# Attention mixer with a four-batch feed-forward: sums of weight blocks distributed over four chunks, in pieces of 256 columns, and three of four early weight loads moved behind a branch

## The chip, the cores and the metric

The kernel runs on one core of one Trainium2 chip. The metric is the device time of one execution in microseconds (us). Three runs of the kernel before gave 744.5, 745.9 and 746.22 us; their median, 745.9 us, is the time before.

## The reference, cut to what matters

```
# attention: q, k, v are [4, 8, 768, 64]; a row sees 4 sink columns and the last 128
scores = where(is_sink | in_window, 0.125 * q @ k.T, -1e9)
x = softmax(scores) @ v                      # heads joined: [4, 768, 512]
# token mixing over the sequence, U [768, 32], V [32, 768]
u = x + ((x.transpose(0, 2, 1) @ U) @ V).transpose(0, 2, 1)
# feed-forward, w_ch1 [512, 2048], w_ch2 [2048, 512]
out = u + relu(u @ w_ch1) @ w_ch2            # all in float32
```

U, V and the weights reach the kernel as 64-bit floats and are narrowed to float32 on the chip.

## The kernel before, in words

The batches go through TensorE one after the other. The attention of batch 0 comes first, alone; then the feed-forward of batch b runs while the attention and the token mixing of batch b+1 are fitted in between its matmuls. Each batch has two chunks of 384 rows, and (b, c) below is chunk c of batch b. A chunk has 16 steps, one for each block f of 128 columns of the hidden layer: 12 matmuls of the first layer (L1251 to L1253) and 9 of the second (L1272). Every operand is split into a high and a low part (two narrow floats whose sum is the float32 value), which is why each product is three matmuls. Chunk 0 takes the blocks in the order 15 to 0, chunk 1 in the order 0 to 15.

Weights: in batch 0 each weight piece (128 x 512 of 64-bit floats) is loaded into one of four `big` buffers, narrowed in seven operations on VectorE (DVE), ScalarE (ACT) or GpSimd (POOL) (`narrow_steps`, L107 to L117), split into high and low parts in a weight tile `w`, and written to DRAM (`wd`). Later chunks fetch `w` from `wd` (1 MB each) into four slots used in turn; blocks 0 and 8 stay resident. A slot gets its next block when all readers of the old one are done.

Batch 3 uses a seven-product scheme (as in Strassen's) for the first layer (`ffn_last`, L1139). It needs, for each pair j of blocks (2j, 2j+1), four combinations of the weights. They are made ahead, in `sums` (L1083 to L1102), while batches 1 and 2 run, and kept in DRAM (`sd`). One sum is: two additions of 128 x 512 that put high and low part of a block together again (L1088, recorded under the helper's lines L514 for DVE and L516 for POOL), four additions or subtractions of 128 x 256 (L1095), one rounding copy of 128 x 1024 (L1097, recorded under L507 for ACT and L508 for DVE), one subtraction of 128 x 1024 for the low part (L1098), and two DMAs of 512 KB to `sd`. Its two tiles `a` and `t` are two of the four `big` buffers, which the output tiles of the chunks use too, strictly in turn. The table `SUMS` (L41) says in which chunk a pair is made; it happens at the step where both blocks of the pair have been fetched.

The order of all instructions on all queues is worked out at build time by a planner (`Plan`): a list scheduler that places some thousands of steps by priority with a cost for each, repeats this with priorities from a backward pass, then tries a few random disturbances (one for each entry of `SEEDS`) and keeps the order with the shortest planned span. SyncE (SP) issues the DMAs in that order and waits at each for what it needs.

Before the planned part the kernel issues some loads by hand (L1579 to L1588): the limits, k and q of the first two head pairs of batch 0, and four weight pieces into the four `big` buffers: U, the two halves of V and the first piece of block 0. Then a branch on the limits chooses between the fast and a general version. What stands behind the branch, the loads of k, q and v of the third head pair and all others included, is issued after it. `narrow` (L525) takes an early buffer if there is one, and otherwise issues a load of its own.

Of the kernel before, what the change touches and what calls it, by code (L numbers as in the profile page):

```python
# [15 lines left out]
U16 = mybir.dt.uint16  # L16
AF = mybir.ActivationFunctionType
ALU = mybir.AluOpType
# [8 lines left out]
DM = H * D  # L27
# [11 lines left out]
K2 = DM // 2  # L39
NPF = NF // 2  # L40
SUMS = {(1, 1): (0, 1, 2, 3), (2, 0): (7, 6, 5, 4)}  # L41
NEG = 8.0e9
# [6 lines left out]
TURNS = 4  # L49
SEEDS = (300012, 300023, 300026,)  # L50
SLACK = 0.0344
# [5 lines left out]
NSTREAM = 4  # L57
NBIG = 4
NNR = 6
NHH = 2  # L60
# [23 lines left out]
def f32(ap):  # L84
    return ap.bitcast(F32)
# [163 lines left out]
class Plan:  # L249
# [116 lines left out]
    def forward(self):  # L366
        avail = dict.fromkeys(self.SYNC, 0.0)
        ready = {e: [] for e in avail}
        dma = port = 0.0

# [33 lines left out]
        while done < len(self.steps):  # L404
# [8 lines left out]
            if pick is None:  # L413
                t, e = turn[0]
                pick = min((s for s in ready[e] if at(s, e) <= t + 1e-9), key=lambda s: (s.prio, s.n))
            s = pick
# [6 lines left out]
            if lock:  # L423
                port = t + s.dur
            avail[e] = t + s.dur
            end = t + s.dur + s.lat
            if e == "SP" and s.lat < 0.0:
                end = -s.lat
                dma = max(dma, end - 1.3)
            elif e == "SP":  # L430
                dma = max(dma, t + s.dur + 0.65) + s.lat
                end = dma + 1.3
# [47 lines left out]
class Fast:  # L480
# [44 lines left out]
    def narrow(self, src, n, prio, dst=()):  # L525

        raw, A, S_ = self.raw(), self.nr(), self.nr()
        if len(self.early) > 0:
            self.early.pop(0)
            self.plan.add("SP", 0.0, lambda: None, w=(raw,), lat=-EARLY[NBIG - 1 - len(self.early)], prio=-1e6)  # L530
        else:
            self.put(raw, lambda: (raw().bitcast(U16)[:, 1:4 * n + 1], src), P * n * 8, prio - 8.0)
        x = self.bank() if dst else None
# [3 lines left out]
        for i, ((ways, r, w), c) in enumerate(zip(steps, cost)):  # L537
            r, w = (box[r],) if r else (), box[w]
            if x and i >= 5:
                r, w = r + (w,), x  # L540
# [542 lines left out]
    def sums(self, j, ws, prio):  # L1083

        a, t = self.raw(), self.raw()
# [10 lines left out]
        hi, lo = (lambda x=x: x()[:, :2 * DM].bitcast(F32R) for x in (a, t))  # L1096
        self.copy(2 * DM, hi, ft, r=(t,), w=(a,), prio=prio)  # L1097
        self.tt(2 * DM, lo, ft, lambda: f32(hi()), ALU.subtract, r=(a,), w=(t,), prio=prio)  # L1098
        sd = self.sd[j]
        for i, (x, y) in enumerate(((a, hi), (t, lo))):  # L1100
            self.put(sd, lambda i=i, y=y: (f32(sd()[:, 2 * i:2 * i + 2].rearrange("p a n -> p (a n)")), f32(y())), 1 << 19, prio,
                     r=(x,), part=i)  # L1102
# [460 lines left out]
def sink_attention_mixer(ctx, tc, q, k, v, vs, limits, U, V, w1, w2, out):  # L1563
# [5 lines left out]
    with tc.tile_pool(name="work", bufs=1) as work, tc.tile_pool(name="idle", bufs=1, space=PSUM) as idle, \  # L1569
# [16 lines left out]
        for src, n in ((U, NB * RANK), (V[0], VC), (V[1], VC), (w1[ORDER[0]], DM))[:NBIG]:  # L1586
            early.append(pre.tile([P, RAW], I32, name=f"big{len(early)}"))
            nc.sync.dma_start(early[-1].bitcast(U16)[:, 1:4 * n + 1], src)  # L1588
        tri = sp.tile([P, 2, P], F32, name="tri")
# [69 lines left out]
```

## Time and profile before

| | |
|---|---|
| median of three runs | 745.9 us |
| the profiled execution | 747.41 us |
| its span, from the first to the last instruction | 745.7 us |
| TensorE (PE) busy | 725.6 us, 97% of the span |
| VectorE (DVE) busy | 494.8 us, 66% |
| ScalarE (ACT) busy | 369.6 us, 50% |
| GpSimd (POOL) busy | 219.8 us, 29% |
| moved by DMA | 157.34 MB, 211 GB/s on average |

In the span the attention of batch 0 fills the first 70 us, batch 0's feed-forward lies from 70.5 to 254.0 us, the chunks (1,0), (1,1), (2,0) and (2,1) begin at 253.96, 345.24, 432.41 and 528.53 us, and batch 3 begins at 612.30 us. Times in all views count from the start of the span. A matmul's recorded duration contains its way through the array, so matmuls that follow one another overlap in the records, and an engine that is busy all the time by the records need not run at its full pace.

### The profile page before, as it was taken

The numbers are of one execution on the slowest core, as the hardware profiler recorded it, in microseconds if no ns is written. First come the engines' busy times: TensorE is split into PE (matmuls) and PEld (weight loads), VectorE is DVE, ScalarE is ACT, GpSimd is POOL, SyncE is SP. The second block draws the span as 40 slices with busy tenths as digits, with TensorE's granted clock in tenths as the row PEclk, the third lists the DMA queues.
The fourth block names the chain that finished last, engine by engine and source line by source line (L and its number), as shares of the span: only waits on it lengthen the run. The fifth ranks groups of instructions, "written<-read, shape, count | busy, mean of one in ns | idle before, by whom it ended". The sixth has DMA issues, their size and how long they took to land.

```text
span 745.7 us, 11814 instructions
## 1 busy us (share of the span) xinstructions
PE 725.6 (97%) x4032; PEld 626.5 (84%) x4032; DVE 494.8 (66%) x1209; ACT 369.6 (50%) x1029; POOL 219.8 (29%) x337
## 2 busy tenths in 40 slices
PE   8989999999998999999999999999999999999997
PEld 7757877778787999999879998898998989888895
DVE  6899889897899567677975198975667224122233
ACT  5996475775874455555543165654545113121220
POOL 4751040313731153353811055754422000000000
PEclk9999999999999999999999999999999999999999
DMA  7559667765795378663599448984157734366433
GB/s 240 157 181 337 245 238 243 267 239 220 227 288 231 129 218 288 185 211 95 171 332 321 173 141 244 350 278 124 72 183 254 239 129 156 133 236 262 173 113 118
DMA packets 46373, 157.34 MB, mean 211 GB/s; under 512 B 5728, under 2 KB 12512, under 8 KB 36576
## 3 DMA queue, kind: packets, MB, share of 16 engines
q1 hardware_dynamic: 46016, 156.11, 61.7%
q8 instruction: 34, 0.56, 0.3%
q10 hardware_dynamic: 288, 0.39, 0.2%
q14 instruction: 35, 0.29, 0.1%
HBM read 116.37 MB, written 40.11 MB: 210 GB/s over the span
## 4 chain that ended last, share of the span: by engine, by line
PE 78%; DVE 9%; ACT 6%; DMA 4%; issue 2%; POOL 2%; SPq 0%; ACTq 0%; DVEq 0%; POOLq 0%
PE bank L1272 23%; PE bank L1209 9%; PE bank L1251 8%; PE bank L1139 8%; PE bank L1252 8%; PE bank L1253 7%; PE bank L693 2%; PE bank L840 2%; PE bank L791 2%; PE bank L717 2%; ACT p L749 1%; PE bank L737 1%; DMA qkraw<-in_q_dram 1%; PE bank L738 1%; DMA v_raw<-in_v_dram 1%
## 5 line engine op out<-in xcount | busy, mean ns | idle before, releaser
L1272 PE MATMUL bank<-w,hh 128*128 128x512 f32 x576 | 184.1, 401 | 0.0
L1251 PE MATMUL bank<-ul,w 128*128 128x384 f32 x384 | 134.2, 350 | 0.7 <-ACT w L507 0.5
L1252 PE MATMUL bank<-uh,w 128*128 128x384 f32 x384 | 129.3, 337 | 0.4 <-DVE w L514 0.3
L1253 PE MATMUL bank<-uh,w 128*128 128x384 f32 x384 | 129.2, 336 | 0.0
L1272 PEld LDWEIGHTS bank<-w,hh 128*128 128x128 f32 x576 | 103.6, 188 | 17.0 <-issue 2.4
L1272 PE MATMUL bank<-w,hl 128*128 128x512 f32 x288 | 114.2, 396 | 1.9 <-DVE hl L1262 1.9
L1262 DVE SCALAR_TENSOR_TENSOR hl<-bank,hh 128x384 fp32r<-128x384 f32 x96 | 53.0, 552 | 58.7 <-ACT hh L1259 58.0
L1259 ACT ACTIVATE hh<-bank 128x384 fp32r<-128x384 f32 x90 | 44.1, 490 | 92.7 <-PE bank L1253 92.2
L749 ACT ACTIVATE p<-p,ms 128x132 f32<-128x132 f32 (+1 forms) x144 | 70.0, 487 | 33.6 <-DVE ms L746 33.4
L1251 PEld LDWEIGHTS bank<-ul,w 128*128 128x128 f32 x384 | 72.4, 188 | 9.4 <-issue 3.4
L1252 PEld LDWEIGHTS bank<-uh,w 128*128 128x128 f32 x384 | 72.3, 188 | 5.1 <-DVE w L514 1.4
L1253 PEld LDWEIGHTS bank<-uh,w 128*128 128x128 f32 x384 | 72.2, 188 | 0.0
L1272 PEld LDWEIGHTS bank<-w,hl 128*128 128x128 f32 x288 | 54.1, 188 | 15.5 <-DVE hl L1262 3.1
L746 DVE CUSTOM_DVE_ANT_0 p<-bank,mask 128x132 f32<-128x132 f32 (+1 forms) x144 | 54.1, 400 | 14.6 <-PE bank L738 9.7
L516 POOL TENSOR_TENSOR p<-p 128x256 f32<-128x256 f32 (+1 forms) x26 | 21.0, 806 | 76.3 <-ACT p L749 75.2
L1170 DVE TENSOR_TENSOR qkraw<-bank,p 128x384 f32<-128x384 f32 x12 | 6.7, 557 | 54.9 <-PE bank L1139 54.9
L1209 PE MATMUL bank<-w,ul 128*128 128x512 f32 x144 | 39.7, 394 | 0.0
L516 POOL TENSOR_TENSOR ul<-xT,uh 128x384 fp32r<-128x384 f32 x9 | 9.1, 1026 | 83.2 <-ACT uh L507 51.7
L507 ACT COPY p<-bank 128x384 f32<-128x384 f32 x16 | 7.7, 478 | 52.0 <-PE bank L1139 52.0
L1209 PEld LDWEIGHTS bank<-w,ul 128*128 128x128 f32 x144 | 26.9, 187 | 6.0
L817 POOL TENSOR_SCALAR_AFFINE_SELECT oph<-oph 128x384 fp32r<-128x384 f32 (+1 forms) x48 | 28.0, 583 | 5.9 <-ACT oph L507 3.1
L791 PE MATMUL bank<-ident,p 128*128 128x128 f32 x144 | 25.8, 279 | 3.6 <-ACT p L773 2.7
(261 smaller groups left out, 1570.2 us busy)
## 6 DMA issues: line engine op xcount, KB each, us to landing
w<-wd SPq DMA_DIRECT2D x52, 1024.0 KB, 5.4
big<-in_w_dram SPq DMA_DIRECT2D x32, 512.0 KB, 4.5
wd<-w SPq DMA_DIRECT2D x16, 1024.0 KB, 4.6
big<-xd SPq DMA_DIRECT2D x33, 256.0 KB, 3.2
sd<-big SPq DMA_DIRECT2D x16, 512.0 KB, 7.2
w<-sd SPq DMA_DIRECT2D x8, 1024.0 KB, 5.0
qkraw<-in_k_dram SPq DMA_DIRECT2D x32, 198.0 KB, 5.5
qkraw<-in_q_dram SPq DMA_DIRECT2D x32, 192.0 KB, 4.6
```

Of the source, the lines that this page charges most:

```text
L516: ways["POOL"] = (gps(n), lambda: nc.gpsimd.tensor_tensor(dst(), a(), b(), op), True)
L746: add("DVE", dve(wd), lambda: nc.vector.tensor_tensor_reduce(p()[:, u, NS + lo:], st()[:, :wd], self.mask[:, min(qb, 2), lo:], -0.125, 3.0 ...
L749: add("ACT", act(wd) + 0.22, lambda: nc.scalar.activation(p()[:, u, NS + lo:], p()[:, u, NS + lo:], AF.Exp, bias=sm()[:, j:j + 1], scale=-1.0,
L791: nc.tensor.transpose(tr()[:, u * P:(u + 1) * P], p()[:, u, SW + NS:], self.ident)
L1139: nc.tensor.matmul(out(), stat(p, dd), mv(dd), start=first and dd == 0 and k == 0, stop=dd == 1 and k == 2, skip_group_check=True)
L1209: nc.tensor.matmul(accs[k](), a()[:, sl], w()[:, m, :], start=False, stop=n == NPF - 1 and f == 1 and q == 2)
L1251: nc.tensor.matmul(ph()[:, :CH], wh, ul()[:, d, :], start=d == 0, stop=False)
L1252: nc.tensor.matmul(ph()[:, :CH], wl, uh()[:, d, :], start=False, stop=False)
L1253: nc.tensor.matmul(ph()[:, :CH], wh, uh()[:, d, :], start=False, stop=d == NC - 1)
L1259: self.plan.any({"ACT": (act(CH), lambda: nc.scalar.activation(hh(), ph()[:, :CH], AF.Relu)), "DVE": (dve(CH), lambda: nc.vector.tensor_sc ...
L1262: add("DVE", dve(CH), lambda: nc.vector.scalar_tensor_tensor(hl(), ph()[:, :CH], 0.0, f32(hh()), ALU.max, ALU.subtract), r=(ph, hh), w=(hl ...
L1272: nc.tensor.matmul(acc[k](), a()[:, sl], w()[:, m, :], start=not begin and i == 0 and j == 0, stop=i == n - 1 and j == 2)
```

## The change

`SUMS` is (1,0): pairs 7, 6; (1,1): pairs 2, 3; (2,0): pairs 5, 4; (2,1): pairs 0, 1, where it was four pairs in (1,1) and four in (2,0). The rounding copy and the low-part subtraction of a sum are four pieces of 256 columns each, with dependencies for each piece, where each was one instruction of 1024 columns. Of the four weight pieces ahead of the branch only U is still loaded there; the loads of both halves of V and of the first piece of block 0 are ordinary planned loads behind it. The planner counts the DMA time of the early loads from its start, and it tries two other seeds in place of three.

```diff
-SUMS = {(1, 1): (0, 1, 2, 3), (2, 0): (7, 6, 5, 4)}
+SUMS = {(1, 0): (7, 6), (1, 1): (2, 3), (2, 0): (5, 4), (2, 1): (0, 1)}
...
-SEEDS = (300012, 300023, 300026,)
+SEEDS = (100004, 100009,)
...
+NEARLY = 1
...
     def forward(self):
...
-        dma = port = 0.0
+        port = 0.0
+        dma = max((-s.lat - 1.3 for s in self.steps if s.lat < 0.0), default=0.0)
...
             if e == "SP" and s.lat < 0.0:
                 end = -s.lat
-                dma = max(dma, end - 1.3)
...
     def narrow(self, src, n, prio, dst=()):
...
-        if len(self.early) > 0:
+        if len(self.early) > NBIG - NEARLY:
...
     def sums(self, j, ws, prio):
...
-        self.copy(2 * DM, hi, ft, r=(t,), w=(a,), prio=prio)
-        self.tt(2 * DM, lo, ft, lambda: f32(hi()), ALU.subtract, r=(a,), w=(t,), prio=prio)
+        for i in range(4):
+            h, l, x = (lambda i=i, v=v: v()[:, i * K2:(i + 1) * K2] for v in (hi, lo, ft))
+            self.copy(K2, h, x, r=[(t, i)], w=((a, i // 2),), prio=prio)
+            self.tt(K2, l, x, lambda h=h: f32(h()), ALU.subtract, r=[(a, i // 2)], w=((t, i),), prio=prio)
...
             early.append(pre.tile([P, RAW], I32, name=f"big{len(early)}"))
-            nc.sync.dma_start(early[-1].bitcast(U16)[:, 1:4 * n + 1], src)
+            if len(early) <= NEARLY:
+                nc.sync.dma_start(early[-1].bitcast(U16)[:, 1:4 * n + 1], src)
```

## Rows read from the trace of the kernel before

**Rows 1.** The page's first two parts: busy time of each engine, and the busy share of DVE in 40 equal slices of 18.6 us.

```profile
PE 725.6 (97%) x4032; PEld 626.5 (84%) x4032; DVE 494.8 (66%) x1209; ACT 369.6 (50%) x1029; POOL 219.8 (29%) x337
...
DVE  6899889897899567677975198975667224122233
```

**Rows 2.** The timeline of PE at the first first-layer matmul of the chunks (1,0), (1,1), (2,0), (2,1) and of batch 3: start, duration, engine, line.

```profile
253.96 0.34 PE L1251 MATMUL bank<-ul,w 128*128 128x384 f32 x1
...
345.24 0.34 PE L1251 MATMUL bank<-ul,w 128*128 128x384 f32 x1
...
432.41 0.34 PE L1251 MATMUL bank<-ul,w 128*128 128x384 f32 x1
...
528.53 0.42 PE L1251 MATMUL bank<-ul,w 128*128 128x384 f32 x1
...
612.30 0.51 PE L1139 MATMUL bank<-kh,w 128*128 128x384 f32 x2
```

**Rows 3.** The busy time of each engine in stretches: start:end and length, then PE, PEld, DVE, ACT, POOL busy with the number of instructions, the granted clock, DMA share and GB/s. The stretches are batch 0's feed-forward and the chunks (1,0), (1,1), (2,0), (2,1).

```profile
70.50:254.00 183.50, 179.45 (x985) 145.92 (x985) 157.94 (x375) 113.08 (x290) 51.41 (x71) 1.00 0.70 241
254.00:345.20 91.20, 91.20 (x544) 84.13 (x543) 65.13 (x180) 53.27 (x174) 37.32 (x70) 1.00 0.62 196
345.20:432.40 87.20, 84.88 (x453) 75.34 (x452) 55.77 (x104) 34.28 (x80) 26.61 (x31) 1.00 0.68 231
432.40:528.50 96.10, 93.82 (x543) 83.79 (x542) 77.81 (x195) 57.28 (x181) 52.19 (x75) 1.00 0.70 221
528.50:612.30 83.80, 83.80 (x456) 75.88 (x455) 41.51 (x85) 29.57 (x69) 18.66 (x28) 1.00 0.55 189
```

**Rows 4.** Who PE waited for, in the chunk (1,1) and then in (2,0): total us, times, longest.

```profile
PE bank L953 <- ACT first1q L507: 0.7, 1, 0.7
PE bank L791 <- ACT p L773: 0.5, 1, 0.5
PE bank L976 <- ACT big L507: 0.5, 1, 0.5
PE bank L936 <- DVE xT L939: 0.4, 1, 0.4
...
PE bank L840 <- POOL oph L817: 1.2, 2, 1.0
PE bank L791 <- ACT p L773: 1.1, 2, 0.9
```

**Rows 5.** The same view as in rows 3 for parts of these chunks: the two parts of (1,1), the two parts of (2,0), and the first part of (2,1).

```profile
345.20:382.00 36.80, 34.69 (x203) 30.21 (x201) 33.19 (x65) 20.16 (x53) 21.31 (x26) 1.00 0.65 210
382.00:432.40 50.40, 50.19 (x252) 45.12 (x251) 22.58 (x40) 14.12 (x28) 5.30 (x5) 1.00 0.71 247
432.40:480.00 47.60, 46.49 (x269) 40.86 (x268) 44.57 (x111) 30.70 (x97) 28.43 (x39) 1.00 0.80 261
480.00:528.50 48.50, 47.33 (x276) 42.94 (x275) 33.23 (x84) 26.57 (x85) 23.76 (x37) 1.00 0.59 181
528.50:580.00 51.50, 51.50 (x295) 47.02 (x294) 35.66 (x75) 25.63 (x61) 16.99 (x27) 1.00 0.55 190
```

**Rows 6.** Groups of instructions by line, engine and shape: count, busy us in total, mean ns of one, idle time before them. The first two are instructions of the sums over the whole span; the next two are two more of the sums, in (1,1) alone; the last is ACT's copy of 384 columns, from 345.2 to 528.5 us.

```profile
L514 DVE TENSOR_TENSOR big<-big,big 128x1024 fp32r<-128x1024 f32 x6 | 7.8, 1292 | 0.2 <-ACT big L507 0.2
...
L507 ACT CAST big<-big 128x1024 fp32r<-128x1024 f32 x6 | 6.3, 1048 | 8.6 <-DVE big L514 5.5 <-POOL opl L814 2.5 <-POOL big L516 0.5
...
L514 DVE TENSOR_TENSOR big<-big,big 128x256 f32<-128x256 f32 x6 | 2.5, 418 | 0.1
L516 POOL TENSOR_TENSOR big<-big,big 128x1024 fp32r<-128x1024 f32 x1 | 2.4, 2402 | 0.0
...
L507 ACT CAST oph<-bank 128x384 fp32r<-128x384 f32 x16 | 7.6, 475 | 3.2 <-PE bank L791 3.1
```

**Rows 7.** DMA issues in (1,0) and then in (2,0): destination and source, count, KB each, median us from issue to landing.

```profile
w<-wd SPq DMA_DIRECT2D x10, 1024.0 KB, 5.2
...
w<-wd SPq DMA_DIRECT2D x10, 1024.0 KB, 7.9
sd<-big SPq DMA_DIRECT2D x8, 512.0 KB, 6.9
```

**Rows 8.** The timeline of SP's DMA issues at the start: start, us until the last of the row was issued, queue, line, destination and source.

```profile
2.67 0.91 SPq L1588 DMA_DIRECT2D big<-in_V_dram  x2
4.18 0.33 SPq L1588 DMA_DIRECT2D big<-in_w_dram  x1
6.34 0.33 SPq L522 DMA_DIRECT2D kh<-in_k_dram  x1
6.73 0.43 SPq L522 DMA_DIRECT2D qs<-in_q_dram  x1
```

**Rows 9.** DMA issues of the first 12 us and then of 13 to 29 us, as in rows 7.

```profile
big<-in_V_dram SPq DMA_DIRECT2D x2, 384.0 KB, 5.5
big<-in_w_dram SPq DMA_DIRECT2D x1, 512.0 KB, 6.0
...
qs<-in_q_dram SPq DMA_DIRECT2D x2, 192.0 KB, 4.7
...
qs<-in_q_dram SPq DMA_DIRECT2D x4, 192.0 KB, 2.9
```

**Rows 10.** The timelines of PE, DVE and ACT where the third head pair of batch 0 begins; in brackets the idle time before and what ended it.

```profile
11.42 2.54 PE L693 MATMUL bank<-kh,qs 64*128 64x132 f32 x12 [1.93 <-ACT p L749]
...
12.20 0.29 DVE L746 CUSTOM_DVE_ANT_0 p<-bank,mask 128x132 f32<-128x132 f32 x1 [1.81 <-PE bank L693]
...
12.65 1.00 ACT L773 ACTIVATE qkraw<-qkraw,r 128x132 f32<-128x132 f32 x3 [1.35 <-DVE r L760]
```

**Rows 11.** The same view as in rows 3 for two stretches of batch 0's attention.

```profile
10.00:15.00 5.00, 3.58 (x17) 2.87 (x18) 3.00 (x20) 3.28 (x14) 2.15 (x5) 0.66 0.87 283
20.00:40.00 20.00, 20.00 (x164) 15.10 (x159) 17.93 (x70) 19.43 (x71) 13.82 (x26) 1.00 0.48 150
```

**Rows 12.** The timeline of DVE at the first reads of the two halves of V and of the first piece of block 0.

```profile
25.62 0.35 DVE L108 TENSOR_SCALAR nr<-big 128x384 uint16<-128x384 uint16 x1
...
37.08 0.35 DVE L108 TENSOR_SCALAR nr<-big 128x384 uint16<-128x384 uint16 x1
...
44.41 0.42 DVE L108 TENSOR_SCALAR nr<-big 128x512 uint16<-128x512 uint16 x1
```

## The prediction

> **What bounds the kernel now.** The page comes first: PE is busy in 97% of the span, and the slices in which DVE is at 8 or 9 tenths lie in the first third, around 350 to 370 us and around 440 to 480 us [rows 1]. So PE sets the time, and a change to DVE, ACT, POOL or DMA work is worth only what it takes from PE's waits. Busy time does not show all of these, because records of matmuls overlap. The better measure here is how long equal PE work takes. The chunks (1,0) and (2,0) do the same work, 544 and 543 matmuls, and last 91.2 and 96.1 us; (1,1) and (2,1) do 453 and 456 and last 87.2 and 83.8 us [rows 2, 3]. The two longer ones are those that hold four sums each. The difference, 4.9 + 3.4 = 8.3 us, is my price of the eight sums as they are placed now, about 1.04 us each. The list of waits agrees in place: PE idles 2.1 us in (1,1) and 2.3 us in (2,0) behind ACT, DVE and POOL work, and in the two chunks without sums it is busy throughout [rows 3, 4]. The rest of the 8.3 us is pace lost under overlapping records. Within (1,1) the loss is all in the first 36.8 us, where the attention and mixing of batch 2 end and DVE is busy 33.2 us; after that DVE is busy 22.6 of 50.4 us [rows 5]. In (2,0) DVE is busy 44.6 of the first 47.6 us [rows 5]. The DMA queue is slower there too: a weight fetch lands 7.9 us after its issue, against 5.2 us in (1,0) [rows 7].
>
> The second limit is the start. Until 70.5 us PE waits on a chain of DVE and ACT work. In it the third head pair begins at 11.42 us after PE idled 1.93 us, DVE 1.81 us, and ACT 1.35 us soon after [rows 10]. The view names ACT as the releaser, but this matmul reads only k and q and needs a PSUM bank that DVE frees. The q load, issued at 6.73 us [rows 8] with 4.7 us to landing [rows 9], lands at 11.4 us, which is when PE starts. So this is a wait for a DMA.
>
> **Part 1, the early loads.** V's two halves (2 x 384 KB) and the first piece of block 0 (512 KB) leave the queue ahead of that k and q. They are issued at 2.67 to 4.5 us [rows 8] and land 5.5 and 6.0 us later, the last about 10.2 us [rows 9]. Loads of the same q size take 2.9 us when less stands ahead [rows 9], so q would land at 6.73 + 2.9 = 9.6 us, 1.8 us earlier. DVE was free at 12.20 - 1.81 = 10.39 us and ACT at 12.65 - 1.35 = 11.30 us [rows 10], so DVE can gain up to 1.81 and ACT 1.35 us. From 20 to 40 us ACT is the fuller of the two, busy 19.43 of 20 us [rows 11], so I take ACT's 1.35 us as what reaches the end of the stage; bounds 0 (the rest of the chain waits for something else) and 1.8 us. PE's granted clock is 0.66 from 10 to 15 us [rows 11], that is partly at the lower of its two levels, after this idle time; less idle time may spare this too, which I don't count. Behind 70.5 us DVE is busy 157.9 of 183.5 us and PE 179.5 [rows 3], so the shift passes through to PE's work.
>
> The three loads are now planned, so SP issues three more DMAs behind the branch, 0.43 us each by its q issue [rows 8]. They can stand behind the k, q and v of the third and fourth pair, and whoever is queued behind them on SP gets its load up to 1.3 us later. Their readers come at 25.6, 37.1 and 44.4 us [rows 12], and even with 6.0 us to landing an issue by 19 us is in time for the first. So I cost them at nothing, under the cover of the attention work up to 25 us; without this cover each us of lateness would be one of DVE's chain. The Trainium skill's page "DMA: Bandwidth & Descriptors", section "Rules for kernel authors", says the opposite of this part: issue a DMA early and wait on it late, so that its fixed cost overlaps. By it the part gains nothing, which is rival D below. The rows speak against it, because these transfers have 15 us or more to spare while a load that is needed at once stands behind them.
>
> **Part 2, where the sums lie.** The work of a sum does not change, its place does. (1,1) keeps the pairs 2 and 3, whose blocks come at its steps 4 to 7. With 87.2 / 16 = 5.45 us a step the first of these pairs is complete at about 345.2 + 5 x 5.45 = 372 us, so most of the work falls into the part where DVE is busy under half of the time [rows 5]: I take 0.5 us for both, against 3.4 now. (2,1) gets two at its start; DVE is busy 35.7 of its first 51.5 us [rows 5], so there is room, but batch 3's mixing lies there: 0.8 us. (1,0) and (2,0) hold two each, at DVE loads between 65.1 in 91.2 us (cost nothing) and 77.8 in 96.1 us (cost 4.9) [rows 3]. If the cost grew in proportion, two sums would cost 2.45 us; if with the square, 1.2. I take 1.85 each, in the middle. New price 0.5 + 0.8 + 1.85 + 1.85 = 5.0 us, gain 8.3 - 5.0 = 3.3 us; bounds 0 (the price stays 1.04 us a sum wherever it lies) and 8.3 us. The change also makes the output tiles of (1,0) and (2,1) wait, on SP, for `big` buffers that sums hold until their DMAs have landed (6.9 us each [rows 7]). These tiles are needed at the chunk's end, some 50 us after the sums, so the feed-forward covers that and I cost it at nothing.
>
> **Part 3, the pieces.** Each sum has three more copies and three more subtractions, 24 of each in all. A 256-column operation takes 418 ns on DVE, so four take 1.67 us against 1.29 us for the one of 1024 columns: +0.38 us [rows 6]. For the copy no 256-column row exists; on ACT it lies between a quarter of 1.05 us and the 0.475 us of 384 columns [rows 6], so four cost between nothing and 0.85 us more; I take 0.35. Eight sums make 8 x 0.73 = 5.8 us of engine time. The sums of (2,0) are 12.7 us of DVE, 4.0 of ACT and 14.9 of POOL, by the differences to (1,0), and cost PE 4.9 us: 0.155 us for one us of engine time [rows 3]. That makes 0.9 us. On the other side a piece frees the engine sooner: now a subtraction of 2.40 us stands on POOL as one block [rows 6], in front of the masks that PE waits for. I take +0.4 us, bounds -0.5 and +0.9. What hides the rest is the feed-forward's matmuls.
>
> The Trainium skill's page "VectorE: DVE Perf Modes", section on the TRN2 errata, speaks against this part: SBUF-source operations pay a fixed cost per instruction, so tile at 512 elements or more. The trace agrees in the price of one (4 x 418 against 1292 ns); if DVE were the bound, this alone would be 8 x 0.38 = 3.0 us, and the sum below would end at 744.2.
>
> **Part 4, the planner.** Other seeds and start values give another order everywhere. No row prices it; it can move small waits either way, and I widen the range by 1.5 us on both sides and add nothing to the sum.
>
> **Sum.** -1.35 - 3.3 + 0.4 = -4.25 us. The profiled execution took 747.41 us with a span of 745.7, so the same execution would come to 743.2. The median of the three runs, 745.9 us, lies 1.5 below it; against the median the forecast is 741.6 us.
>
> **The rivals.** (A) The price of the sums nearly vanishes, because it was only crowding: then -1.8 - 6.9 + 0.2 (the gain of part 2 at 1.4 us left), about 737.5 us. For it: the waits sit in the crowded stretches alone. Against: (1,0) and (2,0) stay fuller than (1,0) is today. (B) The load moves and its price with it: the waits of (2,0) reappear in (1,0), the pieces cost their 0.9 us, and only the start gains: 745.9 - 1.35 + 0.9 = 745.5 us. For it: DVE, ACT and POOL do more work than before. Against: the DVE load of (1,0) would stay below today's of (2,0). (C) Slower: in (1,0) the slots of the blocks 15 to 12 come free only when the additions of the pairs 7 and 6 have read them, and these now queue behind the end of batch 0's narrowing and batch 2's attention. A step is 91.2 / 16 = 5.7 us, the fifth block is needed at about 254 + 4 x 5.7 = 277 us, and its fetch takes 5.2 us or, at today's load of (2,0), 7.9 [rows 3, 7]. From an addition later than 269 us on, each us is one of PE. Four additions that are 2 us late each cost 8 us, against the gain of the start and half of that of part 2: 745.9 + 8 - 1.35 - 1.65 + 0.4 = 751.3 us. Against: in (2,0) the same pairs have the same slots today, and no wait on `w` is in its list [rows 4]. (D) The start gains nothing, because the three loads, once planned, stand in the way of other loads of the attention or reach their readers late: 745.9 - 3.3 + 0.4 = 743.0 us. For it: the DMA share from 10 to 15 us is 0.87 already [rows 11]. Against: from 20 to 40 us it is 0.48, and the readers come late [rows 11, 12].
>
> **How the numbers follow.** Forecast 0.45, A 0.18, B 0.18, C 0.09, D 0.10. A measurement of this kernel can tell about 0.3%, 2.2 us, from no change, so faster means below 743.7 and slower above 748.1 us. Forecast and A are faster, and half of D, which ends close to the bound: 0.68. B and the other half of D are the same: 0.23. C is slower: 0.09. The range leaves C out and reaches from A less 1.0 of the planner's 1.5 us, 736.5, to B with 1.0 of it, 746.5 us.
>
> **What would show it.** Right: the third pair's first matmul near 9.6 to 10 us and batch 0's feed-forward about 1.4 us earlier; (2,0) near 93 and (1,1) near 84.5 us, (1,0) near 93; no wait for a late fetch in (1,0). Wrong, in this order of likelihood: the earlier start is lost again by 70 us; (1,0) takes 95 us or more; the copies on ACT take over 0.5 us; a wait at the end of batch 0 grows because the order there is new.

## The result and the profile after

The change made the kernel slower: 753.85 us (752.62 to 759.1, 6 runs) against 746.06 us for the kernel before, ratio 1.0122, 95% interval 1.009 to 1.0155. The forecast was 741.6 us. The profiled execution took 753.7 us with a span of 752.0 us.

The first view to read is the one of windows, cut where the stages begin. These are the kernel after, in the order batch 0's feed-forward, (1,0), (1,1), (2,0), (2,1), batch 3; the columns are those of [rows 3], which has the rows of before:

```profile
73.50:260.20 186.70, 181.57 (x994) 147.86 (x994) 161.07 (x380) 111.48 (x289) 51.57 (x69) 1.00 0.66 230
260.20:355.40 95.20, 91.81 (x536) 82.46 (x535) 73.39 (x194) 56.44 (x190) 47.55 (x67) 1.00 0.66 213
355.40:438.50 83.10, 83.10 (x453) 75.50 (x452) 45.63 (x96) 31.99 (x76) 25.66 (x33) 1.00 0.65 217
438.50:533.10 94.60, 92.44 (x543) 83.67 (x542) 68.40 (x187) 55.20 (x182) 54.49 (x80) 1.00 0.65 199
533.10:618.00 84.90, 84.15 (x456) 75.91 (x455) 49.17 (x98) 32.82 (x79) 22.59 (x33) 1.00 0.62 214
618.00:752.00 134.00, 128.22 (x634) 113.88 (x632) 36.53 (x65) 27.39 (x56) 0.00 (x0) 0.99 0.47 170
```

By 260.2 us the kernel after is 6.2 us late (254.0 before), and no sum has run yet. (1,0) adds 3.9 us, (1,1) gives back 4.1, (2,0) 1.5; (2,1) and batch 3 lose 1.1 and 0.6. The orders also divide PE's work otherwise: after has 994 matmuls in batch 0 and 536 in (1,0), before 985 and 544. If each matmul is priced at the median time from its start to the start of the next one, for its line and shape in the kernel before (worked out from the trace, not a view), batch 0 holds 2.1 us more work and (1,0) 2.1 us less. So, cleared of moved work, the start loses 3.0 us, batch 0's feed-forward 1.1 and (1,0) 6.1, and (1,1) and (2,0) gain 4.1 and 1.5. Of the 6.3 us by which the span grew, 4.1 are lost ahead of the first sum and 2.2 behind it.

PE's longest waits in (1,0) and then in (2,0); the list of (1,1) is empty, where [rows 4] had four entries:

```profile
PE bank L841 <- POOL oph L818: 2.0, 3, 1.3
PE bank L792 <- ACT p L774: 1.4, 2, 1.0
...
PE bank L841 <- POOL oph L818: 1.6, 2, 1.3
PE bank L738 <- DVE xT L515: 0.4, 1, 0.4
```

These are the two kinds that [rows 4] shows for (2,0) before: a mask on POOL, and on ACT the scaling of the softmax weights. They now stand in (1,0), which had none, with 3.4 us, and the mask in (2,0) as well.

The start, as the timeline of PE at the third head pair, two windows, the second of these windows in the kernel before, and the longest waits of PE from 30 to 73.5 us:

```profile
9.74 0.50 PE L694 MATMUL bank<-kh,qs 64*128 64x132 f32 x4
```

```profile
10.00:15.00 5.00, 4.87 (x40) 3.47 (x38) 4.44 (x28) 4.36 (x19) 3.55 (x7) 1.00 0.94 313
...
40.00:60.00 20.00, 15.14 (x105) 10.31 (x103) 17.77 (x45) 13.76 (x47) 8.08 (x13) 0.83 0.54 184
```

```profile
40.00:60.00 20.00, 17.05 (x111) 10.60 (x112) 18.29 (x49) 16.97 (x56) 9.35 (x15) 0.91 0.60 185
```

```profile
PE bank L718 <- DVE oph L801: 2.9, 1, 2.9
PE bank L718 <- DVE opl L801: 1.9, 1, 1.9
```

The third head pair starts at 9.74 us, 1.68 us earlier, and PE keeps 4.87 of 5 us at clock 1.00 where it had 3.58 at 0.66 [rows 10, 11]. Priced as above, PE has done 1.6 us more work than in the kernel before by 30 us, 0.2 more by 40, the same by 50, 1.6 less by 60 and 3.1 less by 75 us. So the lead is gone by 40 us, without a long wait of PE, and the loss comes behind 50 us; from 40 to 60 us PE is busy 15.14 of 20 us at clock 0.83, against 17.05 at 0.91. DVE's timeline shows what stands in front of the operations that PE waits for at 46.35 and, with the longer wait, at 53.12 us:

```profile
42.12 0.73 DVE L109 TENSOR_SCALAR nr<-big 128x512 uint16<-128x512 uint16 x1
42.77 1.62 DVE L515 TENSOR_TENSOR p<-p 128x384 f32<-128x384 f32 x1
44.32 0.60 DVE L111 TENSOR_SCALAR nr<-nr 128x512 bf16<-128x512 bf16 x1
44.95 0.56 DVE L515 TENSOR_TENSOR vst<-big,vst 32x384 fp32r<-32x384 f32 x1
45.54 0.29 DVE L112 TENSOR_SCALAR nr<-nr 128x512 uint16<-128x512 uint16 x1
45.75 0.55 DVE L801 TENSOR_TENSOR opl<-bank,tri 128x384 f32<-128x384 f32 x1
...
49.79 0.42 DVE L109 TENSOR_SCALAR nr<-big 128x512 uint16<-128x512 uint16 x1
50.12 0.69 DVE L116 SCALAR_TENSOR_TENSOR bank<-big,nr 128x512 f32<-128x512 uint32 x1
50.72 0.55 DVE L515 TENSOR_TENSOR p<-p 128x384 f32<-128x384 f32 x1
51.19 0.87 DVE L515 TENSOR_TENSOR qkraw<-qkraw 128x384 f32<-128x384 f32 x1
51.99 0.54 DVE L801 TENSOR_TENSOR opl<-bank,tri 128x384 f32<-128x384 f32 x1
52.45 0.17 DVE L761 RECIPROCAL r<-r 128x6 f32<-128x6 f32 x1
52.55 0.51 DVE L801 TENSOR_TENSOR oph<-bank,tri 128x384 f32<-128x384 f32 x1
```

Narrowing of weight pieces and of V (L109, L111, L112, L116, `vst`) is drawn ahead of L801, the multiplication with the mask `tri`. PE first reads V at 68.9 us and a weight in the feed-forward at 73.5 us. In front of the second wait the narrowing is 1.0 us and other attention work 1.8 us. The operations are the old ones; their order is new.

### The profile page after: what moved, and what is told of

The parts are those of the page before. It is cut to its first block, busy times and chain, and to the rows that moved or that the text cites. A ratio compares the mean times of both kernels' runs of the same rounds, so it can differ in the third digit from the quotient of the medians.

```text
span 752.0 us, 11925 instructions
## 1 busy us (share of the span) xinstructions
PE 727.5 (97%) x4032; PEld 626.4 (83%) x4032; DVE 499.3 (66%) x1236; ACT 371.2 (49%) x1054; POOL 234.0 (31%) x341
## 4 chain that ended last, share of the span: by engine, by line
PE 73%; DVE 12%; ACT 5%; DMA 4%; issue 3%; POOL 2%; SPq 0%; DVEq 0%; ACTq 0%; POOLq 0%
PE bank L1275 22%; PE bank L1212 8%; PE bank L1142 8%; PE bank L1254 8%; PE bank L1255 7%; PE bank L1256 7%; PE bank L841 2%; DMA w<-wd 2%; PE bank L792 2%; PE bank L718 2%; DMA qkraw<-in_q_dram 1%; PE bank L694 1%; ACT p L750 1%; DVE p L747 1%; ACT qkraw L750 1%
## 5 line engine op out<-in xcount | busy, mean ns | idle before, releaser
L1254 PE MATMUL bank<-ul,w 128*128 128x384 f32 x384 | 134.4, 350 | 0.6 <-ACT w L508 0.4
L750 ACT ACTIVATE p<-p,ms 128x132 f32<-128x132 f32 (+1 forms) x144 | 69.8, 485 | 41.2 <-DVE ms L747 41.1
L1262 ACT ACTIVATE hh<-bank 128x384 fp32r<-128x384 f32 x87 | 42.7, 491 | 94.5 <-PE bank L1256 93.8
L747 DVE CUSTOM_DVE_ANT_0 p<-bank,mask 128x260 f32<-128x260 f32 (+1 forms) x144 | 53.7, 400 | 11.7 <-PE bank L739 7.5
L517 POOL TENSOR_TENSOR p<-p 128x256 f32<-128x256 f32 (+1 forms) x23 | 19.3, 837 | 72.8 <-ACT p L750 64.3
L815 POOL TENSOR_SCALAR_AFFINE_SELECT oph<-oph 128x256 fp32r<-128x256 f32 (+3 forms) x40 | 22.4, 561 | 29.1 <-ACT oph L508 29.0
L818 POOL TENSOR_SCALAR_AFFINE_SELECT opl<-opl 128x384 fp32r<-128x384 f32 (+1 forms) x48 | 28.4, 593 | 6.5 <-ACT opl L508 5.3
```

The lines of the kernel that those rows point to most:

```text
L747: add("DVE", dve(wd), lambda: nc.vector.tensor_tensor_reduce(p()[:, u, NS + lo:], st()[:, :wd], self.mask[:, min(qb, 2), lo:], -0.125, 3.0 ...
L750: add("ACT", act(wd) + 0.22, lambda: nc.scalar.activation(p()[:, u, NS + lo:], p()[:, u, NS + lo:], AF.Exp, bias=sm()[:, j:j + 1], scale=-1.0,
L815: add("POOL", 0.126 + nu * P * 0.914e-3, lambda t=t: nc.gpsimd.affine_select(as_(t()[:, u0:, 0, :]), f32(t()[:, u0:, 1, :]), [[0, nu], [-1 ...
L818: add("POOL", 0.126 + CH * 0.914e-3, lambda t=t: nc.gpsimd.affine_select(as_(t()[:, :, 1, :]), f32(t()[:, :, 1, :]), [[0, NBLK], [1, P]], ...
L1254: nc.tensor.matmul(ph()[:, :CH], wh, ul()[:, d, :], start=d == 0, stop=False)
L1262: self.plan.any({"ACT": (act(CH), lambda: nc.scalar.activation(hh(), ph()[:, :CH], AF.Relu)), "DVE": (dve(CH), lambda: nc.vector.tensor_sc ...
```

## The experiments

"Kept order" means that everything but the named edit stands in the order of the kernel before; "drawn anew" means that the planner ran again. The lengths, in us, lie between the starts of the stages in the one profiled execution of each run; the ratios come from all executions. The start varies by itself: with the kept order and the old loads it is 69.2 to 70.6 us (before, e3, e7, e9, e14, e16).

| run | order | ratio (95%) | start | batch 0 | (1,0) | (1,1) | (2,0) | (2,1) | batch 3 |
|---|---|---|---|---|---|---|---|---|---|
| before | | 1 | 70.5 | 183.4 | 91.3 | 87.2 | 96.1 | 83.8 | 133.4 |
| after | anew | 1.0122 (1.009-1.0155) | 73.5 | 186.6 | 95.2 | 83.1 | 94.6 | 84.8 | 134.0 |
| e1 | kept | 1.0021 (0.9996-1.0046) | 69.5 | 184.0 | 91.3 | 87.0 | 96.4 | 83.5 | 133.9 |
| e2 | after's | 1.0125 (1.0088-1.0161) | 76.0 | 185.8 | 94.8 | 83.1 | 93.2 | 84.9 | 133.3 |
| e3 | kept | 1.0013 (0.9989-1.0036) | 69.8 | 183.4 | 91.3 | 87.1 | 96.1 | 83.6 | 134.2 |
| e4 | anew | 1.0069 (1.0043-1.0095) | 73.8 | 186.2 | 95.2 | 84.0 | 92.4 | 86.0 | 133.3 |
| e5 | anew | 1.0028 (1.0003-1.0054) | 73.6 | 184.2 | 91.0 | 86.4 | 92.0 | 83.5 | 135.1 |
| e6 | anew | 1.0068 (1.0045-1.0092) | 72.6 | 186.2 | 95.0 | 83.1 | 93.4 | 84.6 | 133.2 |
| e7 | kept | 0.9967 (0.9942-0.9992) | 70.6 | 183.3 | 91.3 | 87.4 | 94.8 | 84.6 | 133.3 |
| e8 | after's | 1.0055 (1.0034-1.0076) | 73.5 | 187.7 | 94.7 | 83.1 | 92.8 | 84.8 | 133.3 |
| e9 | kept | 1.0033 (1.0008-1.0057) | 70.6 | 184.2 | 96.9 | 83.2 | 92.3 | 87.6 | 133.5 |
| e10 | anew | 1.0055 (1.0032-1.0077) | 72.4 | 186.8 | 91.1 | 89.6 | 92.9 | 83.6 | 133.4 |
| e11 | anew | 1.0087 (1.0057-1.0117) | 71.3 | 185.9 | 90.5 | 88.7 | 98.3 | 84.5 | 134.5 |
| e12 | kept | 0.9971 (0.9949-0.9993) | 68.1 | 183.3 | 91.3 | 86.9 | 96.4 | 84.3 | 133.5 |
| e13 | kept | 1.0048 (1.0028-1.0069) | 68.3 | 183.1 | 96.7 | 83.2 | 93.9 | 90.1 | 134.2 |
| e14 | e9's | 1.0001 (0.9976-1.0026) | 69.6 | 183.5 | 92.3 | 83.4 | 92.5 | 89.5 | 134.0 |
| e15 | start kept | 1.0052 (1.0029-1.0075) | 70.4 | 189.6 | 97.5 | 83.5 | 93.5 | 85.1 | 133.4 |
| e16 | kept | 0.9980 (0.9957-1.0002) | 69.2 | 183.3 | 91.3 | 85.6 | 93.1 | 83.6 | 135.1 |
| e17 | after's | 1.0101 (1.0072-1.0131) | 74.2 | 186.9 | 94.5 | 83.1 | 91.9 | 84.9 | 136.4 |
| e18 | kept | 0.9996 (0.9974-1.0018) | 67.1 | 183.1 | 91.2 | 83.2 | 94.8 | 87.1 | 134.4 |

**The parts one by one.** e1: the three loads behind the branch, at hand-picked places on SP, all else kept.

```diff
+            if len(early) == 1:
                 nc.sync.dma_start(early[-1].bitcast(U16)[:, 1:4 * n + 1], src)
...
+        for s, after in zip(self.moved[1:], (5, 6, 7)):
+            order.remove(s)
+            sp = [x for x in order if x.eng == "SP" and x not in self.moved]
+            order.insert(order.index(sp[after - 1]) + 1, s)
```

> The kernel before with its order of every instruction on PE, DVE, ACT and POOL kept; only the three early loads (both halves of V, first piece of block 0) are issued behind the branch, after the k and q of the third and fourth head pair. Theory O (the order that the planner drew lost the time, the loads themselves help): the third pair's first matmul at 9.6 to 10 us and 0.5 to 1.8 us less than before, 744.3 to 745.6 us. Rival L (the loads behind the branch stand in the way of later k and q loads and cost the start its 3 us): 748 to 749 us.

The third pair began at 9.46 us instead of 11.42, but the feed-forward only 1.0 us earlier, which is not told from the spread of the start, and no gain in time was measured. The waits of DVE from 10 to 25 us, of e1 and then of e12 (below), tell where it went:

```profile
DVE vsh L508 <- DMA xhl<-in_vs_dram: 2.9, 1, 2.9
```

```profile
DVE vsh L508 <- DMA xhl<-in_vs_dram: 0.3, 1, 0.3
```

The load of `vs` now landed behind the moved ones, and DVE, whose order is fixed, stood 2.9 us for it; the kernel before has no such wait.

e2: the order after, with the three loads ahead of the branch again.

```diff
-            if len(early) <= NEARLY:
+            if len(early) <= NBIG:
```

> The changed kernel with its order kept; only the three loads go back ahead of the branch. Theory O: the loss stays, 753 to 756 us, rather slower than the changed kernel by up to 1.8 us because the third pair waits again. Rival L: about 3 us less than the changed kernel, 750.5 to 751 us, and the first feed-forward matmul at 70.5 us instead of 73.5 us.

The start grew from 73.5 to 76.0 us and the time stayed, as theory O had it: the moved loads are not what cost the changed kernel its time.

e3: the four pieces in place of one instruction.

```diff
-        self.copy(2 * DM, hi, ft, r=(t,), w=(a,), prio=prio)
+        his, los, fts = cut(hi), cut(lo), cut(ft)
+        self.plan.any({"ACT": (act(2 * DM) + 0.07, four(lambda i: nc.scalar.copy(his[i](), fts[i]())), False),
```

> The kernel before with its order kept; each copy and each low-part subtraction of 1024 columns is issued as four of 256 in its place. Theory O: between no change and +0.9 us, 746 to 747 us. Rival P (the small pieces cost what the changed kernel lost): 749 us or more.

No cost that can be told. The four pieces are one step here, one behind the other on one engine, so what separate steps free was not tested. e4 is the changed kernel with the old seeds, e5 the kernel before with `NEARLY = 1` and the planner's new start value, e6 the kernel before with the new `SUMS`; all three are drawn anew.

```diff
-SEEDS = (100004, 100009,)
+SEEDS = (300012, 300023, 300026,)
```

> The changed kernel with the three seeds of the kernel before, so that only the planner's draw differs. Theory O: a draw is worth some us, so it lies 2 us or more away from 753.85 us, and its first feed-forward matmul away from 73.5 us. Rival S (the loss comes with the structure, whatever the draw): within 1 us of 753.85 us.

> The kernel before with only the early-load part of the change (one early load, and the planner's start value for DMA), planned anew with the seeds of before. Theory N (the new order of the start comes from this part, because the planner now fills the start differently): the first feed-forward matmul at 73 us or later and 748 to 753 us. Rival W (the start's new order comes from the sums' new places, through the planner): 70 us and 745 to 747 us.

> The kernel before with only the new table of chunks for the sums, planned anew with the seeds of before; loads and pieces as before. Theory N: the start as before, 70 to 71 us, and the chunks (1,1) and (2,0) shorter, (1,0) and (2,1) longer, 742 to 747 us in all. Rival W: the start at 73 us or later and 749 us or more.

All three reach the feed-forward at 72.6 to 73.8 us, although the edit of e6 touches nothing that runs before 254 us. What they share is that the planner ran again. e4 does not decide between its theories: its median lies 1.9 us from that of the kernel after, and its start is the same. e5 came out as theory N said, e6 close to rival W (72.6 us, 752.2 us); so either edit brings a late start, and neither is needed for one (e10, below).

**The price of the sums.** e7 (order before) and e8 (order after) leave out the sums' arithmetic; their DMAs move a resident weight tile, so batch 3's output is another.

```diff
+        for s in self.plan.steps[mine:]:
+            s.ways = {e: (w[0], lambda: None, w[2]) for e, w in s.ways.items()}
```

> The kernel before with its order kept, the arithmetic of the eight sums left out; the sixteen DMAs to the sums' DRAM tiles stay in their places and move a resident weight tile, so the last batch multiplies other weights. If the prediction's price of 8.3 us for the sums as placed before is right and lies in DVE, ACT and POOL work: 737 to 739 us. If the chunks differ for another reason (their attention and mixing, the DMA traffic): 744 to 746 us.

> The changed kernel with its order kept, the arithmetic of the eight sums left out in the same way. If spread sums cost the predicted 5.0 us: about 749 us. If a sum costs the same wherever it lies: about 745.5 us. If the order is what costs, and the sums little: 752 us or more.

Without any arithmetic of sums (1,1) lasts 87.4 us as before, and the kernel gains 0.33%, 2.5 us, not 8.3. Between e7 and e8 there are still 0.9%, and (1,0) lasts 94.7 us in e8: in the order after, (1,0) stays long without the arithmetic, with the writes still there. The time of e8, 751.06 us, lies between its first case and its last.

**The order.** e10 and e11 are the kernel before with other seeds and nothing else: e10 with the two of the change, e11 with these three.

```diff
-SEEDS = (300012, 300023, 300026,)
+SEEDS = (1, 2, 3,)
```

> The kernel before with nothing but the two seeds of the change, drawn anew. Theory O2 (the order before is a lucky draw, and most orders drawn anew are slower): the feed-forward of batch 0 begins at 72 to 75 us and the time is 749 to 753 us. Rival (only the planner's start value, the new table or the load change lead it to a worse order): begins at 69.5 to 71 us, 745 to 747.5 us.

> The kernel before with three other seeds (1, 2, 3), drawn anew: a second draw of the same lot. Theory O2: the feed-forward of batch 0 begins at 72 to 75 us and the time is 748 to 753 us. Rival: 69.5 to 71 us, 745 to 747.5 us.

Two fresh draws of the same work cost 0.55% and 0.87%. The start of e11, 71.3 us, lies between its two theories, its time above both. e10's start has 2.1 and 1.8 us of PE's waits in two places, e11's 1.8, 1.7 and 1.3; before has none over 1.1 from 20 us on. Priced as above and cleared of moved work, (1,0) begins 2.4 to 4.1 us later than in the kernel before in all six orders that were drawn anew (after, e4, e5, e6, e10, e11), and between 1.5 us earlier and 0.8 us later in the kept ones with the old loads. All of this lies ahead of the first sum.

e9 gives every step that is no part of a sum the priority of the kernel before, and only the sums move; up to some 240 us the order is the one before.

```diff
+            old = Fast(*args)
+            old.run(OLDSUMS)
+            Fast(*args).run(SUMS, old)
...
+            for x, y in zip(rest, was):
+                x.prio = y.prio
```

> The sums move to (1,0), (1,1), (2,0) and (2,1) as in the change, but every other step keeps the priority that it has in the kernel before, so that the order of the start and of batch 0 stays the one before up to about 240 us. Theory O (the loss of the spread table is the newly drawn order, not the sums): batch 0's feed-forward begins at 70 to 71 us and lasts 183 to 184, (1,0) lasts 91 to 93, and the time is 743.5 to 747.5 us. Theory S (the spread places of the sums cost the time themselves): the start as before, but (1,0) lasts 94 to 96 us again and the time is 749 to 752 us.

The outcome lies between the two: start and batch 0 as before (theory O), but (1,0) 96.9 us (theory S), of which (1,1) and (2,0) give most back. PE stands 2.96 us at 312 us in (1,0) for a mask of POOL, this for DVE, and DVE 4.92 us for a DMA:

```profile
312.39 0.91 PE L841 MATMUL bank<-oph,vhl 128*128 128x256 f32 x3 [2.96 <-POOL oph L818]
...
311.81 0.52 POOL L818 TENSOR_SCALAR_AFFINE_SELECT oph<-oph 128x384 fp32r<-128x384 f32 x1 [4.00 <-DVE opl L515]
...
309.08 0.56 DVE L509 CAST qs<-qkraw 128x768 fp32r<-128x768 f32 x1 [4.92 <-DMA qkraw<-in_q_dram]
```

That DMA is a q load of batch 2's attention. e14 keeps e9's order and arithmetic and leaves out the four DRAM writes of the sums 7 and 6.

```diff
+            if j > 5:
+                self.plan.add("SP", 0.5, lambda: None, r=(x,), w=((sd, i),), lat=(1 << 19) / RATE, prio=prio)
```

> e9_spread_kept with the same order on all engines, but the four writes of 512 KB of the sums 7 and 6 to DRAM, which fall into (1,0), are left out; batch 3 reads the sums 5 and 4 in their place, so two sums of the output are others. All arithmetic stays. Theory D (in (1,0) the DMA queue is full, busy at 0.99 to 1.04 from 280 to 310 us, and the loads of batch 2's attention land 9 to 10 us after their issue, for which DVE and then PE wait): (1,0) lasts 91.5 to 94 us against 96.9, the PE wait of 2.96 us at 312 us is under 1 us, time 744 to 747 us. Rival A (the arithmetic of the sums and the order around them cost the time): (1,0) lasts 95.5 to 97 us, time 748 to 750 us.

The window from 280 to 310 us of before, e9 and e14 in turn (the last columns are granted clock, DMA share, GB/s):

```profile
280.00:310.00 30.00, 30.00 (x180) 27.70 (x179) 20.64 (x56) 16.72 (x53) 11.92 (x23) 1.00 0.77 250
```

```profile
280.00:310.00 30.00, 29.43 (x177) 26.98 (x175) 18.54 (x51) 17.86 (x54) 18.88 (x23) 1.00 1.01 315
```

```profile
280.00:310.00 30.00, 30.00 (x183) 27.68 (x182) 20.61 (x56) 17.61 (x55) 19.91 (x25) 1.00 0.83 266
```

The DMA issues of the same stretch, again of before, e9 and e14 (KB each, median us to landing):

```profile
qkraw<-in_q_dram SPq DMA_DIRECT2D x4, 192.0 KB, 4.3
```

```profile
sd<-big SPq DMA_DIRECT2D x3, 512.0 KB, 10.4
qkraw<-in_q_dram SPq DMA_DIRECT2D x4, 192.0 KB, 9.8
```

```profile
qkraw<-in_q_dram SPq DMA_DIRECT2D x4, 192.0 KB, 5.9
```

Theory D holds in this order: with the writes the DMA engines are busy throughout the 30 us (share 1.01), a q load takes 9.8 us to land instead of 5.9 (4.3 before), and (1,0) lasts 96.9 us instead of 92.3. By the ratios the four writes of 512 KB are worth the difference between 1.0033 and 1.0001, whose intervals overlap. DVE, whose load the prediction went by, is less busy in the bad window (18.54) than in the good ones.

e16 and e17 leave out all sixteen writes, in the order before and after.

> The kernel before in its own order, all arithmetic of the sums in place, but none of the sixteen writes of 512 KB of the sums to DRAM; batch 3 reads narrowed weights of the same size in their place, so batch 3's output is another. Theory D (what the sums cost is their writes in the DMA queue, not their arithmetic, which e7_before_without_sums priced at 2.5 us with the writes left in): (1,1) falls from 87.2 to 83.3 to 85 us, (2,0) from 96.1 to 90.5 to 93.5 us, time 738.5 to 743 us, ratio 0.990 to 0.995. Rival A (the writes find room in the queue): (1,1) 86.5 to 87.5, (2,0) 95 to 96.5, time 745 to 747 us.

> The changed kernel in its own order, all arithmetic in place, but none of the sixteen writes of the sums; batch 3 reads narrowed weights of the same size in their place, so batch 3's output is another. Theory D: (1,0) falls from 95.2 to 91 to 93 us, (2,0) from 94.6 to 90.5 to 93 us, the start and batch 0 stay at 73.5 and 186 to 187 us, time 746 to 750 us, ratio 1.000 to 1.005; what then remains over e16_before_no_writes is the order drawn anew. Rival A: (1,0) 94.5 to 95.5, time 751 to 754 us.

In the order before, (1,1) and (2,0) become 1.6 and 3.0 us shorter, where theory D asked for 2.2 to 3.9 and 2.6 to 5.6; the time, 744.17 us, lies outside both ranges. Batch 3 is 1.7 us longer in that execution, and 2.4 us in that of e17, so the fetches that stand in for the sums may have a cost of their own. By the ratios the writes are worth 0.2% with an interval that ends at 1.0002. In the order after, theory D falls for (1,0), which keeps 94.5 us and its waits for POOL and ACT (1.5 and 1.4 us), though (2,0) falls to 91.9; the kernel is still 1.01% over before. So without a single write the two kernels stand at 1.0101 and 0.998. They still differ in the order, the places of the arithmetic, the pieces and the loads, and no run leaves out arithmetic and writes together: why (1,0) is long in the order after stays open.

The table says one thing more. With two sums (1,0) lasts 94.5 to 97.5 us (92.3 in e14), without any 90.5 to 91.3, drawn anew or not; with two sums (1,1) lasts 83.1 to 84.0, with four 85.6 to 89.6. So what these two chunks lose goes with the places of the sums, and what is lost ahead of (1,0) goes with the draw.

The first part of (1,1), 345.2 to 382.0 us, shows the two prices side by side: before [rows 5], without arithmetic (e7), and, for the nearly equal stretch from 345.1, without writes (e16):

```profile
345.20:382.00 36.80, 34.19 (x204) 31.08 (x203) 22.98 (x52) 18.62 (x52) 11.93 (x20) 0.97 0.66 217
```

```profile
345.10:382.00 36.90, 35.73 (x210) 31.62 (x209) 34.02 (x65) 20.15 (x51) 21.98 (x27) 1.00 0.49 157
```

Taking 10 us of work from DVE gained PE nothing (204 matmuls against 203 in the same time); with the writes gone, at a DMA share of 0.49 instead of 0.65, it did 210.

**The loads later, and the whole.** e12 is e1 with the loads behind the k, q and v of the fifth pair.

```diff
-        for s, after in zip(self.moved[1:], (5, 6, 7)):
+        for s, after in zip(self.moved[1:], (12, 14, 16)):
```

> The order before on PE, DVE, ACT and POOL; the three early loads stand behind the branch as in e1_loads_moved, but later on SP, behind the loads of the fifth pair, so that the load of vs and the k and q of the pairs 4 and 5 no longer stand behind them. Theory V (the early gain of 1.9 us was lost to loads that landed late behind the moved ones): third pair at 9.5 us, fifth pair at 19.7 to 20.7 us (21.7 in e1_loads_moved), feed-forward of batch 0 at 68 to 69 us, time 743.5 to 745.5 us. Rival N (the chain of the start waits later for DVE and ACT whatever the loads do): fifth pair 21.5 or later, or the feed-forward at 69.4 to 70.6 us, time 745.5 to 747.5 us.

The start is 68.1 us, 2.4 under before (68.3 and 67.1 in e13 and e18, which place the loads alike), as theory V said, and it reaches the end: 744.31 us (741.5 to 746.7, 12 runs), the only version with all of the work that beats both kernels, by 0.29%, at the edge of what can be told. e13 puts all the change's parts on the order before: e9's spread, e3's pieces, e12's loads.

> What the change does (sums spread, pieces, three loads behind the branch), but on the order before: every step that is no part of a sum keeps its priority, and the three loads stand on SP where e12_loads_later has them. If the parts add up, the ratios 1.0033 (spread), 1.0013 (pieces) and 0.9971 (loads) make 1.0017, 747.2 us. Theory O (about half of the loss of the changed kernel, or more, is the order that was drawn anew at the start and in batch 0): 744.5 to 749 us, feed-forward of batch 0 at 68 to 69 us, (1,0) 94 to 97.5 us. Rival R (the parts of the change together cost what the changed kernel lost, whatever the order): 750 to 754 us.

750.1 us, between the kernels before and after; it is above the range of theory O and just inside that of rival R. The ratio 1.0048 is above the 1.0017 of the parts. The rest up to 1.0122, some 5.5 us, goes with the order drawn anew, in which the loads also stand where the planner put them. The surplus lies in (2,1), 90.1 us against 87.6 in e9; e14 has 89.5 us. PE waits there 2.5 us for ACT's `first1k` and 1.3 for DVE's `hl`, but in e9 2.1 and 1.3 as well, so these waits are not the surplus, and its cause is not known.

e15 takes e6's order from batch 0's feed-forward on and the order before ahead of it.

> The order of e6_spread_only (spread table, drawn anew), but every step that the plan before starts ahead of batch 0's feed-forward has its old priority, so that the start has the order before. Theory O (the 2.1 us that e6_spread_only lost at the start are the new order's, and they pass through to the end): feed-forward of batch 0 at 70 to 71 us (72.6), time 749 to 750.5 us, ratio 1.003 to 1.006. Theory G (an earlier start is given back later, as in e2_after_loads_ahead): at 70 to 71 us too, but the time stays at 751.5 to 753 us.

The start was 70.4 us again, but the time is not measurably better than e6's (1.0052 and 1.0068), and the profiled execution, the longest of its twelve, loses the gain in batch 0 and (1,0). Whether a better start passes through depends on what follows: it did in e12, it did not measurably here. e18 is e12 with a third table.

```diff
+SUMS = {(1, 1): (2, 3), (2, 0): (7, 6, 5, 4), (2, 1): (0, 1)}
```

> The order before with the three loads where e12_loads_later has them, no pieces, and another table: the sums 2 and 3 stay in (1,1), 7, 6, 5 and 4 stay in (2,0), 0 and 1 go to (2,1); (1,0) gets none. Theory D (writes cost where the queue is full, which is while a batch's attention loads: in the first 37 us of (1,1), hardly in (2,1)): (1,1) 83 to 84.5 us (86.9 in e12_loads_later), (2,1) 84 to 86 us, time 740.5 to 744 us. Rival M (the price goes with the sums into (2,1)): (1,1) 83 to 84.5 but (2,1) 87 to 90 us, time 744 to 748 us.

(1,1) fell to 83.2 us as both theories said, and (2,1) rose to 87.1, as rival M said. The median, 745.67 us, is no change; its profiled execution, with 742.52 us, was the shortest of its twelve, so its stage lengths flatter it.

## Why the prediction was wrong

**What bounds the kernel.** PE, as said; that held. The step "The difference, 4.9 + 3.4 = 8.3 us, is my price of the eight sums" failed as a price of work on DVE, ACT and POOL. With the arithmetic gone (1,1) still lasts 87.4 us (e7), with the writes gone 85.6 (e16). Measured, the arithmetic is worth 2.5 us and the writes about 1.5 by ratio (4.6 by the lengths of (1,1) and (2,0)). What the rest is stays open.

**Part 1.** The mechanism was right: third pair at 9.74 us, forecast 9.6 to 10. The size, 1.35 us, was low where the loads stand well (2.4 us in e12). "So I cost them at nothing" failed: in e1 the `vs` load behind them cost DVE 2.9 us. The prediction looked at the readers of the moved loads and not at those of the loads behind them. In the changed kernel the new order had lost the lead by 40 us and 3.1 us more by 75, which is rival D's outcome by another way. The rule that speaks for early loads (the Trainium skill, "DMA: Bandwidth & Descriptors", Rules for kernel authors: issue early, wait late) is not borne out as such here: following it takes the start of the order after from 73.5 to 76.0 us (e2), and leaving it takes that of the order before from 70.5 to 68.1 (e12).

**Part 2.** A gain of 3.3 us was forecast; measured on the kept order is a loss of 0.33%, 2.5 us (e9). The gains came and were larger than forecast: (1,1) and (2,0) became 4.0 and 3.8 us shorter, against 2.9 and 3.05. The failed terms are the prices in the new places, which the prediction took from DVE's load ("I take 1.85 each", "0.8 us"): (1,0) grew by 5.6 us and (2,1) by 3.8. In (1,0) of that order the resource that ran out was the DMA engines (e14); in (2,1) the cause is open. The figure was at hand, 6.9 us for a sum's write [rows 7], but it was used for the release of buffers alone. What e9 shows is a wait behind late loads in (1,0), as in rival C, though of q and not of `w`, and most of the price only moves, as in rival B.

**Part 3.** The forecast was +0.4 us with bounds -0.5 and +0.9; e3 measured 1.0013 (0.9989 to 1.0036), so it can't be told from nothing; the other side, an engine that is free sooner, e3 did not test. The rows after: a piece takes DVE 554 ns in the mean (418 assumed) and ACT 405 ns (between 260 and 475 assumed):

```profile
L515 DVE TENSOR_TENSOR big<-big,big 128x256 fp32r<-128x256 f32 x27 | 14.0, 554 | 0.1
L508 ACT CAST big<-big 128x256 fp32r<-128x256 f32 x26 | 9.5, 405 | 3.7 <-DVE big L515 3.7
```

With POOL idle a piece took DVE 410 to 426 ns, as assumed (see the last section). The rule that speaks against the pieces (the Trainium skill, "VectorE: DVE Perf Modes", the section on the TRN2 errata) agrees with the trace in DVE's price, four times these 410 to 426 ns against 1212 to 1226 ns for the whole subtraction of before with POOL idle, and e3 shows nothing of it in the time.

**Part 4.** This is the step that failed most: "No row prices it; it can move small waits either way", 1.5 us to both sides. The sum held nothing for it. A fresh draw of the same work cost 0.55% and 0.87% (4 and 6.5 us, e10, e11). In the changed kernel the draw is 4.1 us by the start of (1,0), and some 5.5 us by e13 against after, with the different places of the loads in it. With the 4 to 6.5 us of e10 and e11 and the 2.5 us of e9 the sum would have come to 752.4 to 754.9 us without the gain of the start. C's time, 751.3 us, was the nearest of the rivals, for a reason that was not the main one. Why the order before is better than all that were drawn anew is not settled: the runs show that it is, and that each new order loses ahead of (1,0), not that the planner had to miss it. Selection would explain it too: an order that was kept for a good measured time looks better than fresh ones. No run tests that.

## What to carry to other kernels

When a change makes a planner draw a new order, price the draw first: run the old work with other seeds, and test the edit on the old order, step for step. Before moving work into a stage that looks idle by its engines, read the stage's DMA share in slices of 30 us or less, and ask which loads will stand behind the new transfers. The difference between two stages of equal matmuls is no price of the one thing in which they are known to differ until that thing has been taken out.

## What was not expected of the hardware

A DVE operation of one shape and line (128 x 384 with both operands in SBUF, L515 on `p`) took 1.62 us at 42.77 us and 0.55 us at 50.72 us in the same execution. During the slow one POOL was busy for all but 0.1 us. The pieces of the sums show the same: of the 27 subtractions on DVE in the kernel after, the 17 during which POOL was idle took 410 to 426 ns, and the ten during which POOL worked took 531 to 984 ns. Not every operation beside POOL was slow (the one at 50.72 us had POOL beside it for 0.3 us), and no run changed POOL's work alone, so the cause is not shown.

PE's granted clock fell behind an idle time of 2.96 us in e9: 1.00 from 305 to 310 us, 0.69 in the next five, that is partly at the lower of its two levels, and 0.97 in the five after that:

```profile
305.00:310.00 5.00, 4.43 (x27) 3.77 (x25) 0.89 (x2) 1.45 (x4) 1.36 (x4) 1.00 0.99 262
310.00:315.00 5.00, 2.61 (x9) 2.61 (x10) 2.90 (x5) 0.00 (x0) 1.90 (x3) 0.69 0.77 191
315.00:320.00 5.00, 5.00 (x30) 4.59 (x30) 2.69 (x10) 1.95 (x7) 1.02 (x1) 0.97 0.39 94
```
